# Output weights of six heads fetched in 3584-byte runs, and the turn of the attention results that this layout asks for, in a decode step that reads 78 MB

## Chip, cores, metric

One core of a Trainium2 chip. The metric is the device time of the program in microseconds; the kernel before takes 189.97 us (median of 6 runs, 189.7 to 190.29). A profile shows one execution; its span (188.0 us for the kernel before, in a run of 190.18 us) leaves out some 2 us around the program's own instructions.

## The reference, cut to what matters

```python
# B = 2 sequences, one new token each; D = 448, 16 query heads, 8 KV heads, Dh = 256, window W = 4096
q = (layernorm(x) @ wq) ...                       # 16 heads of 256
k, v = the last 4096 rows of the caches, each KV head used by rep = 2 query heads
o = softmax(q k^T / 16) v                         # [B, 16, 1, 256]
return x + o.reshape(B, 1, 4096) @ wo + mlp(layernorm(x))   # wo: [4096, 448], bf16
```

K and V of the window are 2 x 2 x 8 x 4096 x 256 bf16 numbers, 67 MB, read once. `wo` is 3.7 MB.

## The kernel before: what the change touches

The kernel walks through the eight KV heads. For each it loads K, V and the 512 rows of `wo` of its two query heads, all on one DMA queue. VectorE transposes K in four pieces (`kt`); TensorE makes the scores (`sc`), ScalarE the exponentials, VectorE transposes them (`pT`), TensorE multiplies by V (`o`). Heads 0 to 5 then have their result as eight rows of 512 (two partial sums, times two sequences, times two query heads). The kernel multiplies it by `wo` with the 256 dimensions on partitions ("mixing", `psE`, products of 128*2 128x448), so it turns it first. Heads 6 and 7 (`NFIX = 2`) multiply the other way round and need no turn.

```python
    def load_wo(kvh, parts=1):
        w = wo_pool.tile([P, rep, ND * D], BF16, tag="wo", name="wo")
        r0 = kvh * rep * Dh
        win = A_wo[r0 : r0 + rep * Dh, :].rearrange("(h p c) d -> p h (c d)", h=rep, p=P)
        # ... dma_start of w[:, hs, :] from win[:, hs, :]: per partition and query head, 2 rows = 1792 bytes

    def values(i):
        # ... 32 products into po [8, 512]
        o_sb = small.tile([NR, NP * Dh], FP32, tag="o_sb", name="o_sb", bufs=1)
        nc.scalar.copy(out=o_sb[:], in_=po[:])

    def finish(i):                                   # the turn: 4 transposes, then the sum of two halves
        for u in range(NP):
            for c in range(ND):
                nc.tensor.transpose(pqv[:, u, c, :], ov[:, u, c, :], ident_f[0:NR, 0:NR])
        nc.vector.tensor_copy(out=o[:], in_=pqv[:, 0, :, 0:BR])
        # ... add the second half; multiply by the reciprocal of the softmax sum -> oT

    # main loop, i over heads, 4 score pieces a head
            for piece in range(NH):
                s = i * NH + piece
                if s + 1 < NSTEP:
                    turn(s + 1)                      # VectorE: kt of the next piece
                scores(s)
                if s >= 1:
                    turn_p(s - 1)                    # VectorE: pT of the last piece
                # ...
                if piece == 0 and i > 1:
                    close(i - 2)                     # finish (the turn), then mix
        # ... after the pieces: values(i - 1)
```

The softmax here doesn't subtract the row's maximum and nothing guards it: scores larger than these inputs give would overflow.

## Time and profile before

| kernel before | value | from |
|---|---|---|
| time | 189.97 us | 6 runs |
| share of the 16 DMA engines | 97.0% | queue table |
| TensorE, VectorE busy | 77%, 57% | page |
| `wo` in packets of 1792 bytes | 8 x 256 = 2048 | the trace's packet records |
| longest wait of TensorE for V in the last head | 0.22 us | timeline |

The DMA lines, the end of the chain of waits and the end of TensorE's timeline stand in the prediction. Two more views are needed. The page's count of DMA packets, in which the 2048 short `wo` packets are most of those "under 2 KB":

```profile
DMA packets 5652, 77.81 MB, mean 414 GB/s; under 512 B 517, under 2 KB 2569, under 8 KB 2954
```

And the groups by line and shape of the kernel before (busy us, mean ns of one, idle time before them), for the turn, its copy and the only other small fp32 product:

```profile
L440 PE MATMUL den<-sums,ones_f 128*128 128x4 f32 x16 | 2.5, 229 | 0.0
L488 PE MATMUL q<-ident_f,o_sb 8*128 8x8 f32 x24 | 3.8, 265 | 0.0
L465 ACT COPY o_sb<-o 8x512 f32<-8x512 f32 x6 | 3.5, 575 | 36.3 <-PE o L457 36.3
```

The code asks for eight `den` products and gets 16 matmuls; it asks for 24 transposes and gets 24.

### The profile page before, as it was taken

Reading aid. Unit: us, or ns where it says so; the run is one execution under the profiler, and the core shown is the slowest. Engines: PE = TensorE matmul, PEld = TensorE weight load, DVE = VectorE, ACT = ScalarE, POOL = GpSimd, SP = SyncE. Lnnn points to the kernel's source line nnn. Section 1 sums busy time; section 2 is a strip of 40 time slices with the busy share of each in tenths; the row PEclk is TensorE's granted clock in tenths of the full one; section 3 lists DMA queues with packets and bytes.
Section 4 is the critical chain, followed back from the end, with each engine's and each line's share of the span. In section 5 each row is a group of like instructions: output and inputs, shape, how many; then the busy total and the mean of one; then the engine's idle time right before and its main releaser. Section 6 shows DMA issues by size and latency. Waiting matters only on the chain.

```text
span 188.0 us, 2346 instructions
## 1 busy us (share of the span) xinstructions
PE 145.5 (77%) x909; PEld 67.0 (36%) x909; DVE 106.8 (57%) x142; ACT 42.5 (23%) x142; POOL 16.5 (9%) x74
## 2 busy tenths in 40 slices
PE   0395089914989988976997599958996689988983
PEld 0131033811334433432442234313442234434662
DVE  6405397049671976079804991099506993977211
ACT  3005015200062124212331223012421242125101
POOL 7000600300003000300030003000030000000000
PEclk9999558855799999997899999975999999999755
DMA  6999899999999999999999999999999899999990
GB/s 220 421 469 446 380 433 442 439 443 439 432 446 418 420 412 421 448 439 386 472 443 441 397 425 446 425 439 422 436 436 439 380 439 429 453 443 387 424 388 35
DMA packets 5652, 77.81 MB, mean 414 GB/s; under 512 B 517, under 2 KB 2569, under 8 KB 2954
## 3 DMA queue, kind: packets, MB, share of 16 engines
q1 hardware_dynamic: 5636, 77.66, 97.0%
q8 instruction: 7, 0.11, 0.2%
q14 instruction: 3, 0.02, 0.0%
q10 hardware_dynamic: 6, 0.01, 0.0%
HBM read 77.67 MB, written 0.00 MB: 413 GB/s over the span
## 4 chain that ended last, share of the span: by engine, by line
DMA 60%; DVE 19%; PE 16%; SPq 2%; ACT 1%; issue 1%; ACTq 0%; DVEq 0%
DMA k<-in_A_k_cache_dram 50%; DVE kt L386 14%; DMA v<-in_A_v_cache_dram 10%; PE o L457 7%; PE sc L398 4%; DVE pT L424 3%; PE psE L210 3%; PE q L507 1%; SPq L362 1%; ACT p L412 1%; SPq L114 0%; PE psA L227 0%; DVE oT L471 0%; PE q L488 0%; SPq L295 0%
## 5 line engine op out<-in xcount | busy, mean ns | idle before, releaser
L386 DVE STREAM_TRANSPOSE kt<-k 128x2048 f32<-128x2048 f32 x32 | 73.1, 2288 | 49.7 <-DMA k<-in_A_k_cache_dram 49.7
L398 PE MATMUL sc<-kt,qdiag 128*128 128x512 bf16 x256 | 63.9, 401 | 17.2 <-DVE kt L386 17.2
L412 ACT ACTIVATE p<-sc,off 128x256 bf16<-128x256 f32 x64 | 33.0, 545 | 73.3 <-PE sc L398 72.6
L398 PEld LDWEIGHTS <-qdiag 128*128 128x128 bf16 x256 | 24.4, 101 | 56.5 <-issue 23.2
L457 PE MATMUL o<-v,pT 128*8 128x512 bf16 x192 | 42.5, 379 | 0.0
L457 PEld LDWEIGHTS <-pT 128*8 128x8 bf16 x192 | 17.2, 92 | 22.4
L424 DVE STREAM_TRANSPOSE pT<-p 128x512 bf16<-128x512 bf16 x32 | 21.7, 677 | 6.1 <-ACT p L412 6.0
L279 POOL COPY qdiag<-qt 32x16 bf16<-32x16 bf16 x64 | 13.0, 249 | 120.9 <-PE sc L398 104.8
L210 PE MATMUL psE<-wo,oT 128*2 128x448 bf16 x28 | 8.6, 444 | 7.2 <-DVE oT L471 7.2
L412 ACT ACTIVATION_READ_ACCUMULATOR p<-sc,off 128x1 f32 x64 | 11.8, 184 | 0.0
L465 ACT COPY o_sb<-o 8x512 f32<-8x512 f32 x6 | 3.5, 575 | 36.3 <-PE o L457 36.3
L210 PE MATMUL psE<-v,act_bf 128*2 128x448 bf16 x14 | 5.2, 567 | 6.5 <-DVE act_bf L344 6.5
L259 PE MATMUL q_ps<-v,xq 128*128 128x512 bf16 x28 | 8.0, 455 | 2.9 <-DMA v<-in_A_wq_dram 2.9
L507 PE MATMUL q<-pT,v 128*128 128x4 bf16 x256 | 7.2, 168 | 0.2 <-DMA v<-in_A_v_cache_dram 0.2
L507 PEld LDWEIGHTS <-v 128*128 128x128 bf16 x256 | 7.3, 102 | 0.3 <-DMA v<-in_A_v_cache_dram 0.3
L269 DVE CAST q_sb<-q_ps 128x512 bf16<-128x512 f32 x2 | 1.3, 687 | 8.6 <-PE q_ps L259 8.6
L259 PEld LDWEIGHTS <-xq 128*128 128x128 bf16 x28 | 3.1, 112 | 7.7 <-issue 3.5
L210 PEld LDWEIGHTS <-oT 128*2 128x2 bf16 x28 | 2.0, 91 | 10.2 <-DVE oT L471 7.8
L210 PEld LDWEIGHTS <-act_bf 128*2 128x2 bf16 x14 | 1.6, 121 | 9.5 <-DVE act_bf L344 6.5
L488 PEld LDWEIGHTS q<-ident_f,o_sb 8*128 8x128 f32 x24 | 3.3, 207 | 3.0 <-issue 3.0
L180 PE MATMUL xnT_ps<-ident,xn_bf 2*128 2x2 bf16 x7 | 0.5, 166 | 4.7 <-DVE xn_bf L138 4.7
L269 ACT CAST q_sb<-q_ps 128x512 bf16<-128x512 f32 x2 | 1.1, 588 | 12.9 <-PE q_ps L259 12.9
(59 smaller groups left out, 46.0 us busy)
## 6 DMA issues: line engine op xcount, KB each, us to landing
k<-in_A_k_cache_dram SPq DMA_DIRECT2D x7, 4096.0 KB, 29.4
v<-in_A_v_cache_dram SPq DMA_DIRECT2D x7, 4096.0 KB, 29.0
k<-in_A_k_cache_dram SPq DMA_DIRECT2D x2, 2048.0 KB, 24.5
v<-in_B_w_dram SPq DMA_DIRECT2D x2, 1568.0 KB, 24.8
wo<-in_A_wo_dram SPq DMA_DIRECT2D x7, 448.0 KB, 29.7
v<-in_A_wq_dram SPq DMA_DIRECT2D x1, 2048.0 KB, 7.7
v<-in_A_v_cache_dram SPq DMA_DIRECT2D x1, 2048.0 KB, 15.4
v<-in_A_wq_dram SPq DMA_DIRECT2D x1, 1536.0 KB, 10.8
```

Of the source, the lines that this page charges most:

```text
L210: nc.tensor.matmul(psE[:], lhsT=lhsT, rhs=w, start=start, stop=stop, skip_group_check=True)
L259: nc.tensor.matmul(ps[u][:], lhsT=xq[:, s, :, :].rearrange("p j k -> p (j k)"), rhs=wq_sb[:, s, u * N5 : (u + 1) * N5], start=(s == 0), st ...
L269: copy(out=q_sb[:, u * N5 : (u + 1) * N5], in_=ps[u][:])
L279: nc.gpsimd.tensor_copy(out=tv[rows, :, e, j * Q : (j + 1) * Q : HS].rearrange("p n (b h) -> p n b h", b=Bsz), in_=qv[rows, :, h0 : h0 + r ...
L386: nc.vector.transpose(out=kt[:].bitcast(FP32), in_=k[:, half * TH * Dh : (half + 1) * TH * Dh].bitcast(FP32),)
L398: nc.tensor.matmul(psc[:], lhsT=qdiag[i % NW][:, n * NE + e, :], rhs=ktv[:, n, e, :, :], start=(n == 0 and e == 0), stop=(n == NB - 1 and ...
L412: nc.scalar.activation(out=pv[:, b, :, :], in_=sv[:, b, :, :], func=ACT.Exp, scale=scale, bias=off[:, b : b + 1], accum_out=state["rs", i] ...
L424: nc.vector.transpose(out=pT[:], in_=p_t.pop(s)[:])
L457: nc.tensor.matmul(po[:], lhsT=pT_t[i * NH + piece][:, uh * NP * Q : (uh + 1) * NP * Q : HS], rhs=v[:, u * NP : (u + 1) * NP, :].rearrange ...
L465: nc.scalar.copy(out=o_sb[:], in_=po[:])
L488: nc.tensor.transpose(pqv[:, u, c, :], ov[:, u, c, :], ident_f[0:NR, 0:NR])
L507: nc.tensor.matmul(po[:, c, :], lhsT=vv[:, t, c, :], rhs=pTv[:, th, 0:Q:HS], start=(t == 0 and c == 0), stop=(t == T - 1), skip_group_chec ...
```

## The change

The intent: in `wo`, let partition p hold four consecutive rows, 3584 bytes in one run, so that six of the eight loads take half as many packets. Four consecutive rows out of 512 on 128 partitions put the first query head on partitions 0 to 63 and the second on 64 to 127. So the results have to be turned into that shape: ScalarE copies each result row twice (once for each half of the partitions), fp32 products with slices of an identity sum the two partial sums on the way, and a mask `own` keeps on each half the query head that belongs there.

```diff
+            nc.sync.dma_start(
+                out=w[:].rearrange("p h n -> p (h n)"),
+                in_=A_wo[r0 : r0 + rep * Dh, :].rearrange("(p j) d -> p (j d)", p=P),
+            )
+            return                                   # for heads 0 to 5
...
-        nc.scalar.copy(out=o_sb[:], in_=po[:])
+        for u in range(NP):
+            nc.scalar.copy(
+                out=o_sb[:, u, :, :, :],
+                in_=po[:, u * Dh : (u + 1) * Dh]
+                .rearrange("r (m j) -> r j m", j=NJ).unsqueeze(2).to_broadcast([NR, NJ, rep, PH]),
+            )
...
-        for u in range(NP):
-            for c in range(ND):
-                nc.tensor.transpose(pqv[:, u, c, :], ov[:, u, c, :], ident_f[0:NR, 0:NR])
+        for j in range(NJ):
+            for u in range(NP):
+                nc.tensor.matmul(
+                    pqv[:, j, :],
+                    lhsT=o_sb[:, u, j, :, :].rearrange("r h m -> r (h m)"),
+                    rhs=ident_f[0:NR, u * BR : (u + 1) * BR],
+                    start=(u == 0 and j == 0), stop=(u == NP - 1), skip_group_check=True,
+                )
...   # VectorE: times the reciprocal, times own, add the two query heads (three instructions, as before)
```

`own` comes from two reductions of the identity at the start. The mixing stays four products a head.

More of the change, by code (lines that the diff above doesn't have):

```diff
@@ L167 @@
     )
+    PH = P // rep
+    own = consts.tile([P, Bsz, rep], FP32)
+    for h in range(rep):
+        nc.vector.tensor_reduce(
+            out=own[:, :, h],
+            in_=ident[:, h * PH : (h + 1) * PH].unsqueeze(1).to_broadcast([P, Bsz, PH]),
+            axis=AXIS.X,
+            op=ALU.add,
+        )
     ones_f = consts.tile([P, P], FP32)
@@ L353 @@
     NSTEP = Hkv * NH
+    NFIX = 2
     k_t, kt_t, v_t, p_t, pT_t, wo_t = {}, {}, {}, {}, {}, {}
@@ L375, in load_wo @@
         r0 = kvh * rep * Dh
+        wo_t[kvh] = w
+        if kvh < Hkv - NFIX:
+            nc.sync.dma_start(
[3 more added lines that the diff above has]
+            return
         win = A_wo[r0 : r0 + rep * Dh, :].rearrange("(h p c) d -> p h (c d)", h=rep, p=P)
@@ L379, in load_wo @@
             nc.sync.dma_start(out=w[:, hs, :], in_=win[:, hs, :])
-        wo_t[kvh] = w
     def turn(s):
@@ L445, in denominator @@
         return rec
+    NJ = Dh // PH
+    assert rep == 2 and NJ == rep * ND
     NP = 2
@@ L463, in values @@
             )
-        o_sb = small.tile([NR, NP * Dh], FP32, tag="o_sb", name="o_sb", bufs=1)
-        nc.scalar.copy(out=o_sb[:], in_=po[:])
+        o_sb = small.tile([NR, NP, NJ, rep, PH], FP32, tag="o_sb", name="o_sb", bufs=1)
+        for u in range(NP):
+            nc.scalar.copy(
+                out=o_sb[:, u, :, :, :],
+                in_=po[:, u * Dh : (u + 1) * Dh]
+                .rearrange("r (m j) -> r j m", j=NJ)
+                .unsqueeze(2)
+                .to_broadcast([NR, NJ, rep, PH]),
+            )
         state["o", i] = o_sb
@@ L482, in finish @@
     def finish(i):
-        ov = state.pop(("o", i))[:].rearrange("r (u m c) -> r u c m", u=NP, c=ND)
-        pq = ps_q.tile([P, NP * ND * NR], FP32, tag="q", name="q")
-        pqv = pq[:].rearrange("p (u c r) -> p u c r", u=NP, c=ND)
-        for u in range(NP):
-            for c in range(ND):
-                nc.tensor.transpose(pqv[:, u, c, :], ov[:, u, c, :], ident_f[0:NR, 0:NR])
-        o = small.tile([P, ND, BR], FP32, tag="osum", name="osum")
-        nc.vector.tensor_copy(out=o[:], in_=pqv[:, 0, :, 0:BR])
-        for u in range(1, NP):
-            nc.vector.tensor_tensor(
-                out=o[:], in0=o[:], in1=pqv[:, u, :, u * BR : (u + 1) * BR], op=ALU.add
-            )
-        scale_o(i, o)
+        o_sb = state.pop(("o", i))
+        pq = ps_q.tile([P, NJ * BR], FP32, tag="q", name="q")
+        pqv = pq[:].rearrange("p (j r) -> p j r", j=NJ)
+        for j in range(NJ):
[4 more added lines that the diff above has]
+                    rhs=ident_f[0:NR, u * BR : (u + 1) * BR],
+                    start=(u == 0 and j == 0),
+                    stop=(u == NP - 1),
+                    skip_group_check=True,
+                )
+        rec = state.pop(("rec", i))
+        o = small.tile([P, NJ, Bsz, rep], FP32, tag="osum", name="osum")
+        nc.vector.tensor_tensor(
+            out=o[:].rearrange("p j b h -> p j (b h)"),
+            in0=pqv,
+            in1=rec[:].unsqueeze(1).to_broadcast([P, NJ, BR]),
+            op=ALU.mult,
+        )
+        nc.vector.tensor_tensor(
+            out=o[:].rearrange("p j b h -> p j (b h)"),
+            in0=o[:].rearrange("p j b h -> p j (b h)"),
+            in1=own[:].rearrange("p b h -> p (b h)").unsqueeze(1).to_broadcast([P, NJ, BR]),
+            op=ALU.mult,
+        )
+        oT = small.tile([P, NJ, Bsz], BF16, tag="oTm", name="oTm")
+        nc.vector.tensor_tensor(
+            out=oT[:], in0=o[:, :, :, 0], in1=o[:, :, :, 1], op=ALU.add
+        )
+        state["oT", i] = oT
     def values_fixed(i):
@@ L520, in mix @@
         put = add_last if kvh == Hkv - 1 else add
+        if kvh < Hkv - NFIX:
+            for j in range(NJ):
+                add(oT[:, j, :], w[:].rearrange("p h (c d) -> p (h c) d", c=ND)[:, j, :])
+            return
         for h in range(rep):
@@ L527, in mix @@
                 )
-    NFIX = 2
     def close(i):
```

## The prediction

> **What bounds the kernel now.** I read the load of the DMA engines first, then the chain of waits, then the end of TensorE's timeline, because the first two disagree with each other about what sets the end.
>
> The page's slices and queue table, then three stretches of the table by windows (us, busy time of PE, PEld, DVE, ACT, POOL, granted clock, DMA share, GB/s):
>
> ```profile
> DMA  6999899999999999999999999999999899999990
> q1 hardware_dynamic: 5636, 77.66, 97.0%
> ...
> 142.50:163.20 20.70, 16.82 (x80) 7.13 (x78) 17.10 (x18) 4.87 (x17) 0.00 (x0) 1.00 1.00 429
> 163.20:177.00 13.80, 12.34 (x171) 7.38 (x170) 8.99 (x17) 4.88 (x17) 0.00 (x0) 0.96 0.99 420
> 177.00:184.30 7.30, 6.30 (x142) 4.43 (x142) 0.80 (x3) 0.00 (x0) 0.00 (x0) 0.50 0.87 357
> ```
>
> Sixteen DMA engines are full from about 2 us to 184 us of a 188.0 us span, so 77.66 MB is a floor: nothing but fewer bytes, or cheaper packets, shortens it. The chain of waits (start, us, what) agrees, but only just:
>
> ```profile
> 151.87 2.20 DVE kt L386
> 154.07 0.14 issue
> 154.21 1.90 PE sc L398 x8
> 156.11 0.12 PE den L440 x2
> 156.22 7.03 PE o L457 x32
> 163.25 0.02 issue
> 163.26 0.54 SPq L362
> ...
> 163.86 18.50 DMA v<-in_A_v_cache_dram
> 182.36 0.04 issue
> 182.40 1.88 PE q L507 x64
> ```
>
> It names a DMA of V as the releaser of the last 64 products. TensorE's own timeline (start, us) says how close a second bound is:
>
> ```profile
> 165.00 0.64 PE L488 MATMUL q<-ident_f,o_sb 8*128 8x8 f32 x4
> 166.30 0.92 PE L210 MATMUL psE<-wo,oT 128*2 128x448 bf16 x4 [0.66 <-DVE oT L471]
> ...
> 180.34 1.85 PE L507 MATMUL q<-pT,v 128*128 128x4 bf16 x64
> 182.40 1.87 PE L507 MATMUL q<-pT,v 128*128 128x4 bf16 x64 [0.22 <-DMA v<-in_A_v_cache_dram]
> 184.53 0.58 PE L227 MATMUL psA<-wo,oT 128*2 128x112 bf16 x16 [0.26 <-DVE oT L471]
> ```
>
> TensorE waited for that V piece for only 0.22 us. From the K landing at 142.50 us on, TensorE and VectorE hand work to each other with hardly a pause (16.82 and 17.10 us busy of 20.70), so at the end the kernel has two bounds, DMA and the compute chain of the last heads, that tie to about 0.2 us. Before 142.5 us only DMA counts: at each K landing VectorE has idled (7.90 us at 142.53), and a load is issued 15 to 30 us before it lands against some 10 us of its own transfer, so compute may lag by several us without starving the queue.
>
> [...] the 1792 packets of 32,768 bytes take 1213 ns at the median, 27.0 bytes per ns. [...] a 1792-byte packet takes 74 ns [...]; the one 3584-byte packet (b1) takes 140 ns [...]. [...] bf16 128x128 loads of L507 follow each other every 27 ns, the fp32 loads of L488 every 120 ns. [...] eight denominators are written (L440) and sixteen matmuls recorded, while a transpose (L488) is one each (24 of six heads' four).
>
> **The change part by part.**
>
> *Removed.* Six of the eight output-weight loads go from 256 packets of 1792 bytes to 128 of 3584, bytes unchanged. Engine time: 6 x 256 x 74 = 113.7 us becomes 6 x 128 x 140 = 107.5 us; the 6.1 us spread over 16 engines is 0.38 us. That is all the DMA gain there is. Five of the six lie ahead of the K that lands at 142.50 us, so it lands 0.32 us earlier; the last V pieces land 0.38 us earlier.
>
> *Setup.* VectorE gets two reductions of 128 elements per batch entry (about 0.25 us each, from L186 at 278 ns). They delay xq from 7.25 to about 7.8 us; TensorE waits for the weights of q until 8.46 us. Hidden.
>
> *ScalarE.* One 8x512 copy (575 ns) becomes two (1.15 us by the same rate). In the tightest place it starts at 163.27 and TensorE wants the result at 165.00. Hidden with 0.6 us to spare[...].
>
> *VectorE at the turn.* Three small instructions of 0.16 to 0.17 us before, three after. No change. The mixing stays four products of 128x448 a head.
>
> *TensorE at the turn.* This is the cost. Four transposes become eight fp32 products, two passes each: 4 weight loads become 16. At 120 ns a load, the last starts 1.78 us after the first, and its matmul ends some 0.3 us later (45 + 253 ns, from L488 and L440): 2.08 us against 0.64, so +1.44 us, six times, 8.6 us in all.
>
> *What of it is on the path.* Heads 0 to 3: nothing, the next K landing resets the chain. Head 4, at 146.81: the old turn ended at 147.45 and VectorE took it up only at 148.50, so 1.05 us of the 1.44 are slack; the rest, about 0.4 us, delays the transposes of K, then the scores and the values that end at 163.25. Head 5, at 165.00: VectorE already waited there (idle 1.50 us), and TensorE, too, for oT. All 1.44 us pass on, through kt, scores, values and mixing, to the last products.
>
> Sum at the end of the chain: -0.32 (K earlier) + 0.43 + 1.44 - 0.22 (the V wait, which disappears) = +1.33 us. The DMA bound moves down by 0.38 us but no longer matters. 190.18 + 1.33 gives 191.5; I take 191.4, for the clock below.
>
> **The rivals.**
>
> *DMA stays the bound: about 189.8 us.* For it: 97% load, and a chain that is 60% DMA. Against it: the 0.22 us wait. It needs a turn of head 5 no longer than about 0.7 us, that is, products that cost what transposes cost.
>
> *The fp32 passes cost more: 193 to 194.5 us.* In L440 the two loads start 217 ns apart, not 120. If every pass took that (the next load waiting for the matmul before), a turn is 3.6 us, +2.9; on the path 1.9 + 2.9 - 0.5 = +4.3 us, slower by 2.3%. Against it: in L440 the first load lies behind a 512-column product, and from first matmul to the next instruction's is 207 ns for two passes, so 0.10 each; L488 shows loads every 120 ns.
>
> *The clock comes to help: about 190.7 us.* The trace grants 0.50 from 175.98 us on, and the four mixing products at 177.06 take 1.65 us where the same four took 0.92 at 166.30. If the shifted work keeps the full clock some us longer, up to 0.7 us of the loss comes back. Or it falls earlier and costs more. [...] I count 0.1 us for it and put the rest into the range.
>
> **Range and chances.** DMA alone is the floor, 189.8; with slack that I do not see, 190.0 is possible. The upper end, 193.0, holds a pass of up to about 0.17 us or a stalled ScalarE copy. Two per cent faster is 186.4 us, below what the bytes allow: 0.01. Two per cent slower, 194.0, needs the slow passes in full: 0.06. Within: 0.93.
>
> **What would show it.** Right: L516 with 96 matmuls, some 2.1 us from first to last in each head; packets of 3584 bytes at 140 ns, the DMA queue done 0.4 us earlier; VectorE waiting for q at head 4, not only at heads 0 and 5; no wait for V before the last products, and those ending near 185.6 us; the chain of waits passing from the K landing near 142 us through kt, o, q and oT to the end without a DMA. Wrong: the last 64 products still released by the V piece and the span shorter (products cheap), or a turn of 3 us and more, or gaps in the DMA slices, which would mean that the delay reaches the queue.

-0.32 + 0.43 + 1.44 - 0.22 is +1.33 us, all worked out from the trace of the kernel before, and 190.18 + 1.33 gives 191.5. The 0.1 us for the clock, which makes it 191.4, was my estimate; that trace did not show what it rested on.

## The result, and the profile after

The changed kernel takes 191.79 us (median of 6 runs, 191.45 to 193.0) against 189.97 us. Ratios here are the mean time of one kernel's runs over that of the other's of the same rounds, so not quite the ratio of the medians: 1.0111, 95% interval 1.0078 to 1.0144. It is slower by about 1.8 us. A later series gave 191.83 us and 1.0103.

The page's packets and queue, after. The short packets are gone from "under 2 KB", the bytes are the same, and the queue's share of a longer span has fallen:

```profile
DMA packets 4885, 77.83 MB, mean 410 GB/s; under 512 B 517, under 2 KB 1033, under 8 KB 2186
...
q1 hardware_dynamic: 4868, 77.66, 95.8%
```

The groups by line and shape, after. L516 is the new turn: 48 products, 96 matmuls. Its copies by ScalarE cost what a contiguous copy cost (573 against 575 ns), but there are two of them:

```profile
L516 PE MATMUL q<-ident_f,o_sb 8*128 8x4 f32 x96 | 11.7, 249 | 0.0
L486 ACT COPY o_sb<-o 8x512 f32<-8x512 f32 x12 | 6.3, 573 | 36.3 <-PE o L477 36.3
L526 DVE TENSOR_TENSOR osum<-q,rec 128x16 f32<-128x16 f32 x6 | 1.1, 175 | 6.5 <-PE q L516 6.5
```

VectorE now waits for the turn in all six heads (6.5 us in total) where it waited in two (2.5 us). TensorE's timeline of the last heads, after (start, us):

```profile
165.13 1.94 PE L516 MATMUL q<-ident_f,o_sb 8*128 8x4 f32 x16
167.75 1.22 PE L220 MATMUL psE<-wo,oTm 128*2 128x448 bf16 x4 [0.68 <-DVE oTm L539]
168.91 6.72 PE L416 MATMUL sc<-kt,qdiag 128*128 128x512 bf16 x24
...
175.61 3.56 PE L554 MATMUL q<-pT,v 128*128 128x4 bf16 x128
179.42 1.65 PE L220 MATMUL psE<-wo,oT 128*2 128x448 bf16 x4 [0.26 <-DVE oT L498]
...
182.70 3.56 PE L554 MATMUL q<-pT,v 128*128 128x4 bf16 x128
186.51 0.54 PE L237 MATMUL psA<-wo,oT 128*2 128x112 bf16 x16 [0.26 <-DVE oT L498]
```

The last 128 products stand in one piece; the wait for V in their middle is gone. The chain of waits now runs from the K landing at 142.30 us to the end without a DMA, and in the page's shares DMA falls and PE (TensorE) grows (before: DMA 60%, PE 16%):

```profile
DMA 49%; PE 30%; DVE 16%; SPq 1%; issue 1%; ACT 1%; ACTq 0%; DVEq 0%
```

One thing was not in the sum. Compare the stretch that begins at 167.75 with the kernel before: from the start of the mixing to the first products of head 6 it took 173.28 - 166.30 = 6.98 us, and now 175.61 - 167.75 = 7.86 us, for the same instructions. The table by windows of the changed kernel says why; the first number after the busy times is the granted clock:

```profile
164.82:168.23 3.41, 2.73 (x21) 2.11 (x20) 1.05 (x4) 1.07 (x4) 0.00 (x0) 1.00 0.98 423
168.23:171.64 3.41, 3.41 (x10) 1.00 (x8) 3.41 (x3) 0.00 (x0) 0.00 (x0) 0.50 0.91 383
```

TensorE gets half its clock for exactly one window of 3.41 us, right after the window that holds the whole turn and its stall. The kernel before had the full clock from 131.6 to 176.0 us. A second profile of the changed kernel, taken for one of the experiments, has no half-clock window there but one after head 4's turn, from 150.57 to 153.98 us; from the mixing to the next values it took 7.97 us, where the first profile took 7.05. Its span is 189.9 us again.

### The profile page after: what moved, and what is told of

It reads as the page before. It is cut to its first block, busy times and chain, and to the rows that moved or that the text cites. A ratio compares the mean times of both kernels' runs of the same rounds, so it can differ in the third digit from the quotient of the medians.

```text
span 189.9 us, 2498 instructions
## 1 busy us (share of the span) xinstructions
PE 154.0 (81%) x981; PEld 75.0 (39%) x981; DVE 107.7 (57%) x144; ACT 45.4 (24%) x148; POOL 16.5 (9%) x74
## 4 chain that ended last, share of the span: by engine, by line
DMA 49%; PE 30%; DVE 16%; SPq 1%; issue 1%; ACT 1%; ACTq 0%; DVEq 0%
DMA k<-in_A_k_cache_dram 49%; DVE kt L404 12%; PE sc L416 10%; PE o L477 7%; PE psE L220 4%; PE q L516 4%; PE q L554 4%; DVE pT L442 2%; PE psA L237 1%; ACT p L430 1%; PE den L458 0%; SPq L114 0%; DVE osum L526 0%; DVE osum L532 0%; DVE oTm L539 0%
## 5 line engine op out<-in xcount | busy, mean ns | idle before, releaser
L416 PE MATMUL sc<-kt,qdiag 128*128 128x512 bf16 x256 | 64.8, 406 | 13.7 <-DVE kt L404 13.7
L486 ACT COPY o_sb<-o 8x512 f32<-8x512 f32 x12 | 6.3, 573 | 36.3 <-PE o L477 36.3
L516 PEld LDWEIGHTS q<-ident_f,o_sb 8*128 8x128 f32 x96 | 11.1, 186 | 2.5 <-issue 2.5
L516 PE MATMUL q<-ident_f,o_sb 8*128 8x4 f32 x96 | 11.7, 249 | 0.0
L269 PE MATMUL q_ps<-v,xq 128*128 128x512 bf16 x28 | 9.1, 503 | 3.1 <-DMA v<-in_A_wq_dram 3.1
L220 PE MATMUL psE<-v,act_bf 128*2 128x448 bf16 x14 | 4.7, 519 | 6.3 <-DVE act_bf L354 6.3
L220 PE MATMUL psE<-wo,oTm 128*2 128x448 bf16 x24 | 6.4, 397 | 4.1 <-DVE oTm L539 4.1
L526 DVE TENSOR_TENSOR osum<-q,rec 128x16 f32<-128x16 f32 x6 | 1.1, 175 | 6.5 <-PE q L516 6.5
```

The source lines that it names most:

```text
L220: nc.tensor.matmul(psE[:], lhsT=lhsT, rhs=w, start=start, stop=stop, skip_group_check=True)
L269: nc.tensor.matmul(ps[u][:], lhsT=xq[:, s, :, :].rearrange("p j k -> p (j k)"), rhs=wq_sb[:, s, u * N5 : (u + 1) * N5], start=(s == 0), st ...
L416: nc.tensor.matmul(psc[:], lhsT=qdiag[i % NW][:, n * NE + e, :], rhs=ktv[:, n, e, :, :], start=(n == 0 and e == 0), stop=(n == NB - 1 and ...
L486: nc.scalar.copy(out=o_sb[:, u, :, :, :], in_=po[:, u * Dh : (u + 1) * Dh] .rearrange("r (m j) -> r j m", j=NJ) .unsqueeze(2) .to_broadcas ...
L516: nc.tensor.matmul(pqv[:, j, :], lhsT=o_sb[:, u, j, :, :].rearrange("r h m -> r (h m)"), rhs=ident_f[0:NR, u * BR : (u + 1) * BR], start=( ...
```

## The experiments

Theory: the loss is the longer turn of heads 4 and 5, which lie on the compute chain that sets the end; heads 0 to 3 cost nothing, because VectorE waits for the next K anyway (7.90 us at 142.53 in the kernel before) and a delay ends in that wait (the K landing "resets" the chain). Rivals: the loss comes with the new loads, copies or setup (A), or extra TensorE work costs wherever it lies (B). Every kernel below gave a correct result. The times and ratios are each against the kernel before on the same chip.

### The turn in bf16

```diff
-        o_sb = small.tile([NR, NP, NJ, rep, PH], FP32, ...)
+        o_sb = small.tile([NR, NP, NJ, rep, PH], BF16, ...)
-                    rhs=ident_f[0:NR, u * BR : (u + 1) * BR],
+                    rhs=ident_b[0:NR, u * BR : (u + 1) * BR],     # the identity in bf16
```

> Theory (the loss is the length of the turn of heads 4 and 5 on the compute chain that sets the end): eight bf16 products[...] last 0.4 to 0.75 us instead of 1.94; the compute chain falls back behind the DMA, the last products wait for V again, and the time is 189.6 us, ratio to before 0.997 to 0.999. Rival A (the loss comes with the new loads, the two ScalarE copies or the setup, which all stay): 191.6 us, ratio 1.009 to 1.011.

Measured: 189.76 us (189.6 to 190.3), ratio 0.9989 (0.9973 to 1.0005). Loads, copies, masks and setup are all there; the time is that of the kernel before. Rival A falls. TensorE's timeline of this kernel at head 5:

```profile
165.77 0.35 PE L518 MATMUL q<-ident_b,o_sb 8*128 8x4 bf16 x8
166.79 0.92 PE L222 MATMUL psE<-wo,oTm 128*2 128x448 bf16 x4 [0.68 <-DVE oTm L541]
```

The same eight products take 0.35 us instead of 1.94: one matmul each, and weight loads that start every 25 ns instead of every 112. One detail of the expectation failed: in this profile the last products did not wait for V; half-clock windows began at 149.6 and 176.9 us in it.

### Heads 0 to 3 only, heads 4 and 5 only, head 5 only

```diff
-        if kvh < Hkv - NFIX:
+        if long_run(kvh):      # kvh in 0..3; in a second kernel kvh in 4, 5; in a third kvh == 5
```

The other heads keep load, copy and turn of the kernel before.

> New layout and fp32 products for heads 0 to 3 only. Theory: each K landing resets the chain, so these four turns cost nothing, and four long-run loads give 0.25 us: 189.7 us, ratio 0.998 to 1.000. Rival B (extra TensorE work costs wherever it lies, +1.9 us spread over six heads): four sixths of the loss, 191.2 us, ratio 1.006 to 1.008.

> New layout and fp32 products for heads 4 and 5 only. Theory: the whole loss is here, and some more, as only two long-run loads are left: 191.8 to 192.1 us, ratio 1.010 to 1.013. Rival B: two sixths of the loss, 190.6 us, ratio 1.003.

> New layout and fp32 products for head 5 only. Theory: its turn is 1.94 us instead of 0.64, all on the path; some 0.3 us of it are taken by the wait for V that disappears; no K lands earlier. 190.1 + 1.30 - 0.3 = 191.1 us, with half-clock windows 190.9 to 192.0; the difference to the run with heads 4 and 5 is head 4's share, 0.3 to 1.4 us. Rival (the two heads cost alike): 190.9 us or less.

| new layout and turn for | median, us | range | ratio (95%) |
|---|---|---|---|
| heads 0 to 3 | 189.77 | 189.64 to 189.91 | 0.9986 (0.9971 to 1.0) |
| heads 4 and 5 | 192.51 | 191.13 to 193.0 | 1.0113 (1.0081 to 1.0145) |
| head 5 | 191.62 | 189.9 to 191.97 | 1.0067 (1.0037 to 1.0097) |
| all six (the change) | 191.79 | 191.45 to 193.0 | 1.0111 (1.0078 to 1.0144) |

Four of the six turns cost nothing, and the two last cost all of it. Rival B falls. In the kernel with heads 0 to 3, the end looks like that of the kernel before, and TensorE waits for V longer:

```profile
182.32 1.87 PE L580 MATMUL q<-pT,v 128*128 128x4 bf16 x64 [1.01 <-DMA v<-in_A_v_cache_dram]
```

Of the 0.79 us that this wait is longer than before, 0.73 come from the clock: head 6's mixing, ahead of it, had the full clock here and took 0.92 us; in the kernel before it took 1.65. So how closely the two bounds tie differs from run to run.

Head 4's share cannot be read off to better than the scatter of the last two kernels, which is large and comes in steps: spans of 189.2 and 189.3 us in two runs and 190.3 to 191.1 us in four with heads 4 and 5; 188.1 us in one run and 189.7 to 190.1 us in five with head 5. The profile of the former, at head 4, has two half-clock windows:

```profile
141.51:144.92 3.41, 1.16 (x6) 0.28 (x4) 2.18 (x1) 1.05 (x2) 0.00 (x0) 1.00 1.02 442
144.92:148.33 3.41, 3.13 (x8) 1.00 (x8) 3.41 (x5) 0.00 (x0) 0.00 (x0) 0.50 1.02 442
148.33:151.74 3.41, 2.73 (x22) 2.11 (x20) 1.58 (x7) 1.07 (x4) 0.00 (x0) 1.00 0.86 365
151.74:155.16 3.42, 3.42 (x9) 1.00 (x8) 3.42 (x3) 0.00 (x0) 0.00 (x0) 0.50 1.05 450
```

The first follows a wait for K, the second the turn of head 4.

### The clock

From the traces' records I took, for every window of 3.41 us that had the full clock and began between 54 and 177 us, the share of it that products of 448 or 512 columns fill, and the clock of the next window. Each product counts as 0.213 us, an estimate: half of the 0.427 us at which those of 512 columns follow each other in the half-clock windows of the kernel before and the changed one. (At the full clock they start every 0.216 us there, those of 448 columns every 0.188.) In the thirteen traces before the last run: 36 windows under 0.345, all 36 followed by half the clock; 23 from 0.345 to 0.415, 7 of them; 369 above, none. Busy time does not decide: the window at 164.82 was busy for 2.73 us of 3.41, and the next had half the clock; a window at 121.4 us in the kernel with head 5 only was busy for 1.52 us, and the next had all of it. A turn's matmuls have four columns and add nothing to this share, and with its stall of 0.68 us a turn of 1.94 us can take up most of a window of 3.41. The windows are not tied to the program (one begins at 48.77 us in the first profile of the changed kernel and at 48.17 us in the second), so whether one falls on a turn is chance. This is a rule that fits these traces; waits empty a window as well, as that for K did above (1.16 us busy of 3.41).

Two kernels follow from that: the changed kernel once more, for its scatter, and one that does useless large products in the stall.

```diff
+        fill = ps_m.tile([P, 512], FP32, tag="m", name="fill")      # after the eight products of the turn
+        for _ in range(3):
+            nc.tensor.matmul(fill[:], lhsT=ident[:], rhs=wo_t[i][:].rearrange("p h n -> p (h n)")[:, 0:512], start=True, stop=True)
```

> The changed kernel unaltered, for a second profile and more times beside those of this call. Theory: the six profiles so far show windows of 3.41 us in which TensorE gets half its clock, each after a window in which the 448- and 512-column products filled less than about 0.37 of the time; a turn of 1.94 us with its stall of 0.68 us can empty a window when the window falls on it. So the times scatter: near 191.2 us (the sum of the prediction) when the chain of heads 4 and 5 meets no such window, up to 193 us when it meets two; median 191.8. Rival (the scatter is that of the chip): before scatters as much.

> The changed kernel with three useless 128x512 products (0.65 us) between each turn and its mixing, where TensorE stalls 0.68 us anyway; the result is not read. Theory of the clock: a window that holds a whole turn is then filled to about 0.41 instead of 0.22, so no half-clock window follows a turn of heads 4 and 5: faster than the changed kernel in spite of more work, 191.2 us (191.0 to 191.5), and none of the times near 193. Rival (the clock falls for another reason, or the scatter is the chip's): same as the changed kernel or up to 0.2 us slower, scatter as before.

> The filled kernel once more, because its profile fell on its one slow run (193.16 us), in which the half-clock windows began in a wait for K, before any turn. Theory: again most times lie near 191.1 us (190.6 to 191.5), 0.7 us below the changed kernel, and the profile of a usual run shows no half-clock window between 142 and 175 us. Rival (the first five fast times were luck): a median of 191.8 us.

Measured: the changed kernel 191.83 us (191.67 to 192.81), while before scattered from 189.81 to 190.51. Filled: 191.12 us (190.64 to 193.16), ratio 1.0069; again: 190.7 us (190.54 to 193.21), ratio 1.0036 (1.0022 to 1.005), against 1.0103 (1.0083 to 1.0122) of the unfilled kernel. More work, less time, as the theory says and the rival does not. In the spans of the single runs the steps are plain: the changed kernel has 189.0 or 189.1 us in two of twelve runs, 189.8 to 190.1 in nine, 190.8 in one; the filled one 188.7 to 189.3 in ten of twelve.

The expectation "none near 193" failed, twice: in both series the run with the profile was the slow one (spans 191.3 and 191.4 us). Its trace shows another door to the same mechanism (TensorE of the filled kernel, first series):

```profile
124.50 2.85 PE L416 MATMUL sc<-kt,qdiag 128*128 128x512 bf16 x8 [2.07 <-DVE kt L404]
127.28 3.57 PE L516 MATMUL q<-ident_f,o_sb 8*128 8x4 f32 x16
130.78 1.46 PE L526 MATMUL fill<-wo,ident 128*128 128x512 bf16 x3
```

A wait for K left the window from 121.9 to 125.3 us at 0.34, so the turn of head 3 itself ran at half the clock, took 3.57 us, and the clock stayed low for three windows; head 3's delay then outlasted the next K landing. But at heads 4 and 5 both of these traces show what was meant: the windows that hold the turns are filled to 0.41 or more, and the clock is full from 135.5 to 179.8 us, turns of 1.94 us included. I have no profile of a usual filled run: that it has no half-clock windows at all on its way is inferred from its times (189.9 us less the 0.88 us of one window is 189.0, an estimate) and from its higher granted clock (0.912 to 0.927 in the ten runs, 0.881 in the two slow ones; 0.874 to 0.899 in the unfilled kernel).

### Short runs with the new turn

```diff
-            nc.sync.dma_start(out=w[:].rearrange("p h n -> p (h n)"), in_=...)     # 128 packets of 3584 bytes
+            rows = A_wo[r0 : r0 + rep * Dh, :].rearrange("(p h c) d -> p h (c d)", p=P, h=rep)
+            for u in range(rep):
+                nc.sync.dma_start(out=w[:, u, :], in_=rows[:, u, :])               # 2 x 128 of 1792 bytes
```

> The changed kernel, but each of the six loads fetched in two halves of 1792-byte runs, 256 packets as before; the data and all else the same. Theory: DMA is not the bound any more; only the K that lands near 142.3 us comes up to 0.32 us later and shifts the chain: 192.0 us, 0.2 to 0.3 above the changed kernel. Rival A (the long runs themselves cost): falls to about 190.0 us.

Measured: 191.72 us (191.09 to 193.16), ratio 1.01 (1.0071 to 1.013). Rival A falls a second time. The 0.2 to 0.3 us of the expectation drown in the steps of the clock. The profile shows one step more. It has the half-clock window after head 4's turn, as the second profile of the changed kernel has, but the half clock of the last stretch begins at 181.1 us instead of 177.9, so head 6's mixing had the full clock, 0.92 us instead of 1.65:

```profile
179.59 0.92 PE L220 MATMUL psE<-wo,oT 128*2 128x448 bf16 x4 [0.26 <-DVE oT L497]
```

The span is 189.2 us instead of 189.9. The changed kernel's two runs of 189.0 and 189.1 us have nearly the granted clock of this one (0.887 against 0.888), so they may be this step and not a run whose turns met no half-clock window; no trace of them tells. Nor is it known whether some filled runs gained here too.

### Head 5's turn done twice

```diff
+        for again in range(2 if i == Hkv - NFIX - 1 else 1):
             for j in range(NJ):
                 ...                                  # the same eight products
```

> The changed kernel with the sixteen passes of head 5's turn done twice. Theory: every pass of head 5 is on the path: 16 x 0.112 = 1.79 us more than the changed kernel, and a half-clock window after it in nearly every run: 193.6 to 194.3 us, ratio to before 1.019 to 1.023. Rival (a turn of another length would be hidden): as the changed kernel.

Measured: 195.06 us (193.38 to 195.97), ratio 1.0253 (1.0218 to 1.0287). Nothing of it is hidden, but the expectation was too low: the doubled turn took 3.73 us, 1.79 more as expected, and cost 3.2 us by the medians of the same series. In its profile, which is that of the fastest run, the window from 166.4 us on has no large product at all, the mixing that follows takes 1.65 us instead of 0.92; the spans of the six runs go from 191.5 to 193.7 us. I read the rest as the clock; the single runs have no trace to show it.

### The turn moved, in fp32, in bf16, and in the kernel before

```diff
-                if piece == 0 and i > 1:
-                    close(i - 2)
+                if piece == NH - 2 and i > 1:
+                    finish(i - 2)
+                if piece == NH - 1 and i > 1:
+                    mix(i - 2)
```

> The changed kernel with the fp32 turn of a head moved behind the third score piece, when the last transposes of K are already recorded on VectorE, and the mixing behind the fourth, so that neither VectorE nor TensorE waits for the turn. Same work. Theory: the turn falls into TensorE's pauses for kt and the stall of 0.68 us before the mixing goes; head 5's values start near 173.8 us instead of 175.6; the end is DMA's again or within 0.5 us of it: 189.9 us (189.5 to 190.5), ratio 0.998 to 1.003. Rival B: the work costs wherever it lies, 191.7 us, ratio 1.010.

> All six long-run loads, the turn in bf16 and behind the third score piece, the mixing behind the fourth. Theory: the compute chain is 1 us or more shorter than the DMA, so DMA alone sets the end and the whole 0.38 us shows: 189.7 us, ratio 0.997 to 0.999, scatter under 0.5 us, and the last products wait for V by 0.5 us or more. Nothing better is to be had, because the bytes are the floor.

> The kernel before, with its transposes behind the third score piece and the mixing behind the fourth: the schedule of the run before this one without the long runs. Theory: the kernel before is bound by DMA to within 0.2 us, so a shorter compute chain gives nothing: 190.0 us, ratio 0.999 to 1.001; against it the long runs stand alone, 0.3 to 0.4 us. Rival (the better schedule is what gains): as fast as the bf16 version.

| turn behind the third piece | median, us | range | ratio (95%) |
|---|---|---|---|
| changed kernel, fp32 | 190.67 | 189.94 to 191.43 | 1.0025 (1.0006 to 1.0044) |
| changed kernel, bf16 | 189.82 | 189.49 to 190.12 | 0.999 (0.9975 to 1.0005) |
| kernel before | 189.82 | 189.71 to 189.91 | 0.999 (0.9977 to 1.0004) |

The same fp32 work in another place costs, by the ratios, a quarter of what it did: rival B falls again. (The values that the expectation calls head 5's are head 6's; they began at 174.59 us, not near 173.8.) TensorE of the moved fp32 kernel:

```profile
164.45 5.41 PE L416 MATMUL sc<-kt,qdiag 128*128 128x512 bf16 x24
169.78 1.94 PE L516 MATMUL q<-ident_f,o_sb 8*128 8x4 f32 x16
171.66 1.91 PE L416 MATMUL sc<-kt,qdiag 128*128 128x512 bf16 x8
173.50 0.92 PE L220 MATMUL psE<-wo,oTm 128*2 128x448 bf16 x4
```

No pause is left, and no half-clock window between 49 and 178 us. The median is a little above the expected 189.9. In the profile head 4's turn and mixing now stand in front of head 5's values without a pause to fill, and head 7's pieces begin at 164.45 us instead of 163.29.

The last two kernels are bound by DMA: in their profiles the last products wait 0.61 and 0.89 us for V. They differ in the length of the runs of `wo` and in the turn that goes with it, and their medians do not differ: the 0.3 to 0.4 us that the expectations gave to the long runs did not show. No version beats the kernel before by more than the noise; 189.76 to 189.82 us are the best medians seen.

### What the long runs are worth

By the traces' packet records, the 16 engines spend 182.08 us each on the queue's packets (those of 4 bytes left out) before and 181.72 us after: 0.36 us less. But from the landing of the second K (before any `wo`) to the last landing it is 144.65, 144.65 and 144.50 us in the three traces with short runs in all heads, and 144.27 to 144.57, mean 144.43, in the eight with six long ones: 0.17 us less, with a scatter as large. About half of the saved engine time became idle engine time before the end; why, these runs do not show.

## Why the prediction was right

The time (191.79 us in 190.0 to 193.0, forecast 191.4) and the mechanism were right. Step by step, by the two profiles:

- *Setup and ScalarE hidden*: right. TensorE still waited for the weights of q by 3.1 us in total (2.9 before), and the two copies ended at 164.44, before the turn at 165.13.
- *The turn, 2.08 us*: 1.94. The loads follow each other at 0.112 us, not 0.120, so it adds 1.30 instead of 1.44.
- *Heads 0 to 3 free*: right, shown by the kernel that changes only them.
- *K earlier by 0.32*: 0.20 in this pair of traces; 0.38 at the last landing was about 0.17. The packet cost was right (74 and 140 ns again); that engine time saved is landing time saved was the wrong step.
- *Head 4, +0.43*: +0.29 (from the K landing until VectorE takes up head 4's turn it is 6.29 us, before 6.00).
- *Head 5, all on the path*: right, 165.13 to 167.75 is 2.62 us, before 1.30.
- *The V wait absorbed, 0.22*: 0.38 (the last 128 products with what follows them, from 3.97 to 3.59 us).
- *The clock, "I count 0.1 us for it" as a gain*: the wrong sign. It cost 0.88 us in the profiled run. The prediction named this as possible ("Or it falls earlier and costs more") but looked only at the stretch from 175.98 us on; the window after the turn was not in its sum. The longer turn helped to empty that window, though a turn is not the only way to an emptied one: in the bf16 kernel, the window with head 4's turn of 0.35 us and a stall of 1.97 us was followed by half the clock too. The hoped-for gain is real as well, but came in other runs: the 0.92 us of head 6's mixing above. In the two profiles compared here it took 1.65 us both times.

The measured terms add up: -0.20 + 0.29 + 1.32 + 0.88 - 0.38, and 0.07 in small pieces, is 1.98 us, the shift of VectorE's last oT (184.31 to 186.29). Without the clock's 0.88 it is 1.10 us, where the prediction summed 1.33: the turn was shorter and the V wait longer than thought. The forecast lies 0.4 us below the measured median because the clock term had the other sign, and those two partly made it good. Part of that nearness is luck: the sum started from 190.18 us, the one profiled run; from the median, 189.97 us, it gives 191.2 us.

Of the rivals, "DMA stays the bound" needed a turn of 0.7 us; the bf16 turn of 0.35 us is that case, and its time was 189.76 against the 189.8 that this rival named. "The fp32 passes cost more" did not come: the pitch in `den` of 0.217 us is not that of a series.

## What to carry to other kernels

A DMA share of 97% is no proof that the compute engines have slack: here, in the profile, a compute chain tied with DMA to 0.2 us, and a longer turn that was free in four heads was fully paid in the last one. Before adding work, look how long the last wait for a transfer is, and where after the last landing that resets the chain the work will stand. Count small fp32 products by the matmuls and weight loads that the trace records, not by columns: here 48 products of four columns were 96 matmuls, 0.112 us apart, and eight of these products took 1.94 us where eight in bf16 took 0.35. And put them between large products rather than next to a stall: here a stretch of tiny products and stalls went before 3.41 us at half the clock, and the same turns between large products took the ratio from 1.0111 to 1.0025.
